# Two weight conversions spread over GpSimd and ScalarE, their raw halves in late token buffers, and three q blocks rotated as one piece

## The chip, the core and the metric

The kernel runs on one core of a Trainium2 chip. The metric is the device time of one execution in microseconds. Lower is better. The five engines of the core are named as in the profile: PE (TensorE; PEld is its weight load), DVE (VectorE), ACT (ScalarE), POOL (GpSimd) and SP (SyncE, which here only issues DMAs).

## The reference, cut to what matters

Attention with rotary position embedding, for 4 batches of 8 heads with 576 positions of 64 channels, and a gated feed-forward layer on its output:

```python
q_rot, k_rot = (rotate(q), rotate(k))
scores = scale * np.matmul(q_rot, k_rot.transpose(0, 1, 3, 2))
scores = scores - np.max(scores, axis=-1, keepdims=True)
attn = np.exp(scores); attn = attn / (np.sum(attn, axis=-1, keepdims=True) + 1e-09)
x = (attn @ v).transpose(0, 2, 1, 3).reshape(2304, 512)
g = x @ w_gate                       # 512 x 1536, random normal
return (g / (1 + np.exp(-g)) * (x @ w_val)) @ w_out
```

The weights of the layer are 64-bit floats. The kernel loads them as pairs of 32-bit words and turns each pair into a 32-bit high part and a low part. This is the conversion that the change is about.

## The kernel before

All products are made from pairs of a high and a low part (fp32r), so each score block takes several matmuls. The kernel has two phases.

**Attention, 0 to 285 us.** The 32 heads are worked in 16 pairs. A pair has nine score blocks of 128x576: n counts blocks over the whole phase, p is the pair and b the block in it (n = 9p + b). For each block PE multiplies (`scores`, L347), DVE takes the negated row maximum (`peak`, L362), ACT takes the exponential (`exp`, L380), PE transposes the result (L423), ACT rounds the transpose to its high part (L424) and DVE subtracts to get the low part (L425). PE then multiplies with v (`pv`, L463), ACT copies the result to Y and SP stores it. Beside this POOL rotates q and k of pair p+2 (`rope`, L200 to L202) and splits v (`vsplit`, L276 and L277). PE transposes the rotated pair p+1 (L287, L291); ACT and DVE split it into the tile N (L306, L310), and SP copies N into the stacked tiles QK, QZ and BD, eight DMAs a pair (`qk_stack`, L317 to L324), which the scores of pair p+1 read. There are two N, QK, QZ and BD, used in turn. From pair 5 on POOL also turns attention outputs that came back from DRAM (Xab, by two DMAs for each piece) and the reciprocal sums (R) into tokens for the second phase (`xprep`, L631 to L634).

**The feed-forward layer, from 285 us on.** It is not touched by the change, but for the two tiles named below that it uses.

The two conversions in the attention phase are for the first block of `w_gate` (i = 0) and of `w_val` (i = 1). `conv` begins each at the first block number of its row in `cv` (the load of the 128x1024 words), and issues one step at each further block number. The steps before are: absolute value (ACT, L733), clamp (DVE, L734), shift (DVE, L735), merge of the exponent into the word (DVE, L736), mask (DVE, L737), rounding to the high part (ACT, L709), product of the low word with the scale (DVE, L738), subtraction and addition (POOL, L711 and L712). All work on 128x512 elements in one tile of the pool `m_r`, which holds a single buffer, named R. The same buffer takes the reciprocal sums later, so the first load of R waits for the last step of the second conversion (L712).

**What sets the order.** PE's order is written out to block 9, SP's to block 46, POOL's to the end of the attention phase. Elsewhere a scheduler places instructions by its own model of time, among what the steps issue. All engines run their streams in order. A DMA on SP also waits until the eighth DMA before it has landed, since they share eight semaphores in turn. All these DMAs go through one queue (q1 in the profile).

The first pair has its own code (`start`): k and block 0 of q are rotated on DVE, the other blocks of q on POOL, with a table that ACT scales first.

Of the kernel before, what the change touches and what calls it, by code (L numbers as in the profile page):

```python
# [10 lines left out]
FP32 = mybir.dt.float32  # L11
F32R = mybir.dt.float32r
U32 = mybir.dt.uint32
ACTF = mybir.ActivationFunctionType
ALU = mybir.AluOpType
AX = mybir.AxisListType

B, H, S, D = 4, 8, 576, 64
# [20 lines left out]
    rope=1,  # L39
    vsplit=8,  # L40
    rstore=0,
    cv=[[9, 13, 14, 15, 16, 17, 17, 19, 24, 24], [28, 36, 37, 38, 39, 40, 40, 42, 44, 44]],
    xs=[[5, 1], [5, 5], [6, 5], [7, 5], [8, 7], [9, 5], [10, 5], [11, 5], [12, 7], [13, 7], [14, 1], [14, 2],
        [14, 8], [15, 0], [15, 2], [15, 4]],
    xe=[[5, 4], [6, 3], [7, 3], [8, 3], [9, 3], [10, 3], [11, 3], [12, 3], [13, 5], [14, 1], [14, 3], [14, 5],
        [15, 1], [15, 3], [15, 5], [15, 7]],
    c1=[[3, 3, 4, 4, 5, 5, 6, 6, 6], [7]],
)
# [39 lines left out]
def bits_f32(x):  # L88
    return float(np.array([x], np.uint32).view(np.float32)[0])


W_LO = bits_f32(896 << 20)
W_HI = bits_f32((1151 << 20) - 1)


def r32(ap):
    return ap.bitcast(FP32)
# [10 lines left out]
class Attn:  # L108
# [101 lines left out]
    def start(self):  # L210
        nc = self.nc
        ve, po = nc.vector, nc.gpsimd
        rot = self.rot[0] = self.rot_p.tile([128, NSLOT, D], FP32, name="rot")
        rf = rot.rearrange("p s d -> p (s d)")
        T = nc.tensor.transpose
        tr = lambda: self.tr_p.tile([128, 512], FP32, name="tr")
        hi = lambda *x: self.qk_hi(0, *x)
        lo = lambda *x: self.qk_lo(0, *x)
        pw = self.pv_p.tile([128, 512], FP32, name="pv")

        def warm(n):
            for _ in range(n):
                nc.tensor.matmul(pw[:, 0:128], self.ident, self.ident, start=True, stop=True)
        w = PLAN["warm"]
        nc.scalar.copy(self.et_p.tile([128, 640], FP32, name="Et")[:, 0:1], r32(self.BD[0])[:, 0, 0:1])
        warm(w[0])
        self.turn(po, 0, 2)
        tp = self.sc_p.tile([128, 1024], FP32, name="sc").rearrange("p (s d) -> p s d", d=D)
        self.turn(ve, 0, 1, 0, 4, tp[:, 0:8])
        nc.scalar.mul(self.tab[0], self.tab[1], float(D ** -0.5))  # L230
        nc.scalar.copy(tp[:, 8:10], self.tab[0][:, :, 0])
        self.turn(ve, 0, 0, 0, 1, tp[:, 10:12], tp[:, 8:10, None])
        self.turn(po, 0, 0, 1, 2)
        self.turn(po, 0, 0, 2, 4)
        pk, pt, pq = tr(), tr(), tr()
        kt = lambda i: T(pk[:, i * 128:(i + 1) * 128], rf[:, 512 + i * 128:640 + i * 128], self.ident)
        for o in (64, 0):
            T(pt[:, o:o + 128], rf[:, 1024:1152], self.ident)
        warm(w[1])
        for i in range(4):  # L240
            kt(i)
        warm(w[2])
        T(pq[:, 0:128], rf[:, 0:128], self.ident)
        for x in ((pt, None, 192), (pk, 640, 512), (pq, 64, 128)):
            hi(*x)
        for x in ((pt, None, 192), (pk, 640, 512), (pq, 64, 128)):
            lo(*x)
        nc.scalar.copy(self.VS[0][:, :, 0:64], self.VR)
        warm(w[3])
        self.scores(0, False, lambda x: warm(w[4]) if x == 0 else None)  # L250
        self.peak(0)
        T(pq[:, 128:256], rf[:, 128:256], self.ident)
        self.scores(1, False)
        self.peak(1)
        hi(pq[:, 128:256], 192, 128)
        self.exp(0)
        lo(pq[:, 128:256], 192, 128)
        self.exp(1)
        warm(w[5])
        self.scores(2)  # L260
        ps = tr()
        for i in range(2, 4):
            T(ps[:, i * 128:(i + 1) * 128], rf[:, i * 128:(i + 1) * 128], self.ident)
        hi(ps[:, 256:512], 320, 256)
        lo(ps[:, 256:512], 320, 256)
        self.exp(2)
        del self.rot[0], self.X[0]
        self.load_qk(2)
        self.qk_stack(0)
# [231 lines left out]
BK = 384  # L501
# [4 lines left out]
class Moe:  # L506
# [197 lines left out]
    def bits10(self, raw, X, hi, lo):  # L704
        nc, po = self.nc, self.nc.gpsimd
        Hf, Xf = r32(raw)[:, :, 1], r32(X)
        ops = self.bits(raw, lo, po, Xf, Xf)
        return ops[:5] + [
            lambda: nc.scalar.copy(hi, Hf),  # L709
            ops[5],  # L710
            lambda: po.tensor_tensor(out=Hf, in0=Hf, in1=r32(hi), op=ALU.subtract),  # L711
            lambda: po.tensor_tensor(out=lo, in0=Hf, in1=Xf, op=ALU.add),  # L712
        ]
# [31 lines left out]

    def wfirst(self, f, i):
        if f == 0:
            tmp = self.r_p.tile([128, 1536], U32, name="R")
        else:
            tmp = self.again("raw0", [128, 1536], U32, "raw")  # L750
        self.nc.sync.dma_start(out=tmp[:, 0:1024], in_=self.wsrc(i, f))
        raw, X = tmp[:, 0:1024].rearrange("p (f t) -> p f t", t=2), tmp[:, 1024:1536]
        if f == 0:
            return self.bits10(raw, X, *self.Wb[f][i])
        go = lambda Xt=None: self.bits9(raw, X, *self.Wb[f][i], self.nc.gpsimd, Xt)
        return (lambda: go(self.aux())) if i else go()
# [215 lines left out]
def attn_swiglu(ctx: ExitStack, tc: tile.TileContext, qk, vr, wg, wv, wo, main, tail, out):  # L972
    nc = tc.nc
# [7 lines left out]
    moe = Moe(tc, keep, pl, yd, rd, hd, wg, wv, wo, out)  # L981
# [3 lines left out]
    ve, po = nc.vector, nc.gpsimd  # L985
# [75 lines left out]
    @step  # L1061
    def x(n, p, b):
        if [p, b] in P["xs"]:
            s, c, t = xq.pop(0)
            need = {8 * s + c, ("r", 2 * s)} | ({4 + c, ("r", 1)} if t else set())
            assert need <= at.done
            if c == 0:
                moe.rload(s, t)
            pend.append((s, c, t, moe.xload(s, c, t)))
        if [p, b] in P["xe"]:  # L1070
            moe.xprep(*pend.pop(0), po)
# [9 lines left out]
    P, cvq, cv1 = PLAN, [], {}  # L1081
# [4 lines left out]
    for n in range(NB):  # L1086
        p, b = divmod(n, 9)
# [24 lines left out]
    ps = [moe.mm(0, 0, 0, 0)]  # L1112
# [9 lines left out]
    ps = [moe.mm(0, 0, 1, 0)]  # L1122
# [258 lines left out]
```

## Time and profile before

| | us |
|---|---|
| median of 3 runs (723.10 to 726.07) | 725.21 |
| the profiled execution | 726.19 |
| its span | 724.4 |

So 1.79 us of the profiled execution lie outside its span, and it is 0.98 us above the median. Over the span PE is busy 97%, DVE 75%, POOL 65% and ACT 57%. The clock that PE was granted is 0.99 of full speed over the span, and 1.00 in every stretch of the attention phase. A pair begins here with its first row maximum on DVE. From pair 7 on most pairs take close to 16.5 us; the earlier ones take between 15.6 and 20.3 us.

### The profile page before, as it was taken

How to read it: one execution, taken by the hardware profiler on the slowest of the kernel's cores; microseconds unless marked ns; L12 is line 12 of the kernel's file. 1: busy time of each engine (PE TensorE's matmuls, PEld its weight loads, DVE VectorE, ACT ScalarE, POOL GpSimd, SP SyncE). 2: the span in 40 equal slices, each digit the busy share in tenths (PEclk: the TensorE clock that was granted, in tenths of full speed). 3: DMA queues.
4: the chain of work that ended last, by engine and by line, in shares of the span. 5: the costliest groups of instructions: out<-in, count | busy, mean ns of one | idle time of the engine just before them, and what ended most of it. 6: DMA issues, size and time to landing. Idle time of an engine off the chain costs nothing.

```text
span 724.4 us, 12748 instructions
## 1 busy us (share of the span) xinstructions
PE 699.1 (97%) x4342; PEld 656.5 (91%) x4342; DVE 541.7 (75%) x889; ACT 409.9 (57%) x891; POOL 472.8 (65%) x473
## 2 busy tenths in 40 slices
PE   7999988999999999997999999999999999999997
PEld 6889988999999998997999999999999877888887
DVE  5798897888888888657998878778667794465451
ACT  5788987888888887346543433415243332432331
POOL 8879699999999858576986766555765767200000
PEclk9999999999999999998999999999999999999999
DMA  4887799779887896873357565745648964787661
GB/s 156 204 226 202 201 235 218 209 206 243 223 224 193 212 217 193 220 248 114 116 150 215 157 177 151 201 133 171 183 122 256 312 231 157 307 279 231 203 218 30
DMA packets 111329, 143.86 MB, mean 199 GB/s; under 512 B 17808, under 2 KB 86048, under 8 KB 111264
## 3 DMA queue, kind: packets, MB, share of 16 engines
q1 hardware_dynamic: 106576, 137.64, 66.6%
q10 hardware_dynamic: 4688, 5.39, 2.2%
q8 instruction: 35, 0.57, 0.3%
q14 instruction: 30, 0.25, 0.1%
HBM read 76.35 MB, written 42.54 MB: 164 GB/s over the span
## 4 chain that ended last, share of the span: by engine, by line
PE 69%; DMA 11%; DVE 8%; ACT 5%; POOL 3%; issue 2%; SPq 2%; ACTq 0%; DVEq 0%; POOLq 0%
PE ch L822 28%; PE ch L939 13%; PE pv L463 9%; PE sc L347 8%; PE tr L423 6%; DMA HF<-hf 3%; PE ch L890 2%; DMA QK<-N 2%; PE tr L287 1%; DMA ht<-sv 1%; ACT E L380 1%; DMA yd<-Y 1%; DMA R<-rd 1%; DVE HF L880 1%; PE ch L774 1%
## 5 line engine op out<-in xcount | busy, mean ns | idle before, releaser
L362 DVE TENSOR_REDUCE nmt<-sc 128x1 f32<-128x576 f32 x144 | 108.2, 752 | 24.4 <-PE sc L347 23.6
L380 ACT ACTIVATE E<-sc,nmt 128x576 f32<-128x576 f32 x128 | 97.1, 759 | 4.5 <-DVE nmt L362 4.5
L423 PE MATMUL tr<-ident,E 128*128 128x128 f32 x512 | 77.2, 273 | 1.1 <-DVE ET1l L425 0.9
L806 POOL TENSOR_TENSOR u<-u,z 128x384 f32<-128x384 f32 x30 | 30.5, 1017 | 71.3 <-DVE sg L806 65.7
L423 PEld LDWEIGHTS tr<-ident,E 128*128 128x128 f32 x512 | 61.4, 141 | 3.9 <-PE tr L287 1.2
L347 PE MATMUL sc<-QK 128*128 128x288 f32 x240 | 58.7, 326 | 4.1 <-DMA QK<-N 2.4
L825 ACT COPY c<-ch 128x384 f32<-128x384 f32 x30 | 14.4, 480 | 84.3 <-PE ch L822 50.2
L200 POOL TENSOR_TENSOR t<-X,tab 128x256 f32<-128x256 f32 (+2 forms) x96 | 55.5, 600 | 6.3 <-DMA X<-in_qk_dram 2.7
L424 ACT CAST ET2h<-tr 128x512 fp32r<-128x512 f32 x80 | 47.0, 588 | 18.0 <-PE tr L423 17.9
L425 DVE TENSOR_TENSOR ET2l<-tr,ET2h 128x512 fp32r<-128x512 f32 x80 | 53.3, 684 | 4.2 <-ACT ET2h L424 3.9
L682 DVE TENSOR_TENSOR hl<-hg,hh 128x384 fp32r<-128x384 f32 x44 | 25.8, 587 | 38.5 <-ACT hh L682 38.5
L939 PE MATMUL ch<-Oh,hh 128*128 128x512 f32 (+1 forms) x144 | 54.0, 375 | 0.0
L939 PE MATMUL ch<-Ol,hh 128*128 128x512 f32 (+1 forms) x144 | 53.8, 374 | 0.0
L939 PE MATMUL ch<-Oh,hl 128*128 128x512 f32 (+1 forms) x144 | 53.8, 374 | 0.0
L347 PE MATMUL sc<-N,QZ 128*128 128x288 f32 x240 | 51.6, 297 | 0.0
L202 POOL TENSOR_TENSOR rot<-rot,t 128x512 f32<-128x512 f32 (+2 forms) x48 | 47.3, 985 | 3.8
L425 DVE TENSOR_TENSOR ET1l<-tr,ET1h 128x512 fp32r<-128x512 f32 x64 | 42.9, 685 | 5.7 <-ACT ET1h L424 5.4
L201 POOL TENSOR_TENSOR rot<-X,tab 128x512 f32<-128x512 f32 (+2 forms) x48 | 47.2, 983 | 0.0
L806 DVE TENSOR_TENSOR sg<-ch,u 128x384 f32<-128x384 f32 x60 | 33.4, 557 | 16.5 <-PE ch L822 13.0
L682 ACT CAST hh<-hg 128x384 fp32r<-128x384 f32 x44 | 22.6, 514 | 38.9 <-DVE hg L926 38.9
L424 ACT CAST ET1h<-tr 128x512 fp32r<-128x512 f32 x64 | 36.9, 595 | 12.1 <-PE tr L423 11.8
L347 PEld LDWEIGHTS sc<-QK 128*128 128x128 f32 x240 | 36.9, 190 | 7.4 <-ACT E L380 3.4
(417 smaller groups left out, 2416.4 us busy)
## 6 DMA issues: line engine op xcount, KB each, us to landing
QK<-N SPq DMA_DIRECT2D x64, 288.0 KB, 4.8
hg<-ht SPq DMA_DIRECT2D x22, 768.0 KB, 6.7
HF<-hf SPq DMA_DIRECT2D x12, 896.0 KB, 5.8
X<-in_qk_dram SPq DMA_DIRECT2D x15, 576.0 KB, 6.4
yd<-Y SPq DMA_DIRECT2D x31, 256.0 KB, 3.3
ht<-sg SPq DMA_DIRECT2D x20, 384.0 KB, 3.6
hf<-sg SPq DMA_DIRECT2D x20, 384.0 KB, 3.4
ht<-sg SPq DMA_DIRECT2D x20, 320.0 KB, 2.9
```

The lines of the kernel that those rows point to most:

```text
L200: e.tensor_tensor(out=sel(t2, u), in0=sel(x, w), in1=tb(Sn, u), op=ALU.mult)
L347: nc.tensor.matmul(ps[:, g, 0:288], l, rr[:, o + g * 288:o + (g + 1) * 288], start=(x == 0), stop=(x == len(terms) - 1))
L362: nc.vector.tensor_reduce(out=nmcol, in_=ps[:, :, 0:288], axis=AX.XY, op=ALU.max, negate=True)
L380: nc.scalar.activation(out=E.rearrange("p (a b) -> p a b", a=2), in_=ps[:, :, 0:288], func=ACTF.Exp, bias=nmcol, scale=1.0, accum_out=self ...
L423: nc.tensor.transpose(ps[:, c], E[:, o + c * 128:o + (c + 1) * 128], self.ident)
L424: nc.scalar.copy(dst[0], src)
L425: nc.vector.tensor_tensor(out=dst[1], in0=src, in1=r32(dst[0]), op=ALU.subtract)
L463: nc.tensor.matmul(st["ps"][:, 0:w], VS[:, sl, :], t, start=(x == 0), stop=(x == last))
L682: return [lambda: self.nc.scalar.copy(h, f), lambda: le.tensor_tensor(out=l, in0=f, in1=r32(h), op=ALU.subtract)]
L806: add = lambda e, out, in0, in1: e.tensor_tensor(out=out, in0=in0, in1=in1, op=ALU.add)
L822: nc.tensor.matmul(acc, l[:, w, c * 128:(c + 1) * 128], r, start=(n == 0), stop=(n == 5))
L939: self.nc.tensor.matmul(ps, l[:, f], r[:, z], start=(n == 0), stop=(n == 3 * NFF - 1))
```

## The change

It has three parts.

1. **Conversion (`bits10`).** The clamp moves from DVE to POOL. The product is taken apart: ACT scales the low word by 2^-52 in place, right after the absolute value, and POOL multiplies. DVE keeps three steps: shift, merge and mask. `cv` gets one more step for each conversion, and the steps move: the first conversion's shift, merge and mask go from blocks 15, 16 and 17 to 18, 21 and 25, the second's from 38, 39 and 40 to 30, 34 and 39. The second conversion's load moves from block 28 to block 20.
2. **Buffers.** The raw words lie in the slots `xa1h` and `xa1l`, tiles for tokens of the third piece (needed from pair 12 on), and no longer in R. The first load of R and of Xab moves from pair 5, block 1 to pair 4, block 6, and the first `xprep` one block earlier.
3. **Start.** ACT scales the small part of the table for block 0 into a PSUM tile of its own (`td`) before it scales the whole table. POOL rotates blocks 1 to 3 of q in one piece. PE transposes them together, and ACT and DVE split them in one 128x384 piece each, in place of one of 128 and one of 256 columns.

```diff
-    cv=[[9, 13, 14, 15, 16, 17, 17, 19, 24, 24], [28, 36, 37, 38, 39, 40, 40, 42, 44, 44]],
-    xs=[[5, 1], [5, 5], ...
+    cv=[[9, 13, 13, 14, 18, 21, 22, 25, 26, 26, 26], [20, 24, 25, 26, 30, 34, 35, 39, 44, 44, 44]],
+    xs=[[4, 6], [5, 5], ...
-    xe=[[5, 4], [6, 3], ...
+    xe=[[5, 3], [6, 3], ...
...
-        tp = self.sc_p.tile([128, 1024], FP32, name="sc").rearrange("p (s d) -> p s d", d=D)
+        tp, td = (self.sc_p.tile([128, 1024], FP32, name="sc").rearrange("p (s d) -> p s d", d=D) for _ in range(2))
         self.turn(ve, 0, 1, 0, 4, tp[:, 0:8])
+        nc.scalar.mul(td[:, 0:2], self.tab[1][:, :, 0], float(D ** -0.5))
         nc.scalar.mul(self.tab[0], self.tab[1], float(D ** -0.5))
-        nc.scalar.copy(tp[:, 8:10], self.tab[0][:, :, 0])
-        self.turn(ve, 0, 0, 0, 1, tp[:, 10:12], tp[:, 8:10, None])
-        self.turn(po, 0, 0, 1, 2)
-        self.turn(po, 0, 0, 2, 4)
+        self.turn(ve, 0, 0, 0, 1, tp[:, 8:10], td[:, 0:2, None])
+        self.turn(po, 0, 0, 1, 4)
...
-        T(pq[:, 128:256], rf[:, 128:256], self.ident)
+        ps = tr()
+        for i in range(1, 4):
+            T(ps[:, i * 128:(i + 1) * 128], rf[:, i * 128:(i + 1) * 128], self.ident)
         self.scores(1, False)
+        hi(ps[:, 128:512], 192, 384)
+        lo(ps[:, 128:512], 192, 384)
         self.peak(1)
-        hi(pq[:, 128:256], 192, 128)
         self.exp(0)
-        lo(pq[:, 128:256], 192, 128)
...
-        ps = tr()
-        for i in range(2, 4):
-            T(ps[:, i * 128:(i + 1) * 128], rf[:, i * 128:(i + 1) * 128], self.ident)
-        hi(ps[:, 256:512], 320, 256)
-        lo(ps[:, 256:512], 320, 256)
...
-        return ops[:5] + [
+        return [
+            ops[0],
+            lambda: nc.scalar.mul(r32(L), L, 2.0 ** -52),
+            lambda: po.tensor_scalar(out=Xf, in0=Xf, scalar1=W_LO, scalar2=W_HI, op0=ALU.max, op1=ALU.min),
+            ops[2], ops[3],
             lambda: nc.scalar.copy(hi, Hf),
-            ops[5],
+            ops[4],
+            lambda: po.tensor_tensor(out=Xf, in0=r32(L), in1=Xf, op=ALU.mult),
             lambda: po.tensor_tensor(out=Hf, in0=Hf, in1=r32(hi), op=ALU.subtract),
...
-            tmp = self.r_p.tile([128, 1536], U32, name="R")
+            tmp = self.again(f"xa1{'hl'[i]}", [128, 1536], U32, "raw")
...
+            if (s, t, c) == (0, 2, 0):
+                assert not cvq
+                moe.xa[1] = [moe.again(f"xa1{x}", [128, 4, BK], F32R, f"xa1{x}") for x in "hl"]
```

On PE at the start, before (L347 are the scores of blocks 0, 1 and 2, L252 the transpose of q's block 1, L263 those of blocks 2 and 3, L423 the first transposes of exponentials, L223 filling matmuls):

```order
L347 MATMUL sc<-N_93 128x288 x6
L252 MATMUL tr<-ident,rot 128x128
L347 MATMUL sc<-N_93 128x288 x6
L223 MATMUL pv<-ident 128x128
L347 MATMUL sc<-N_93 128x288 x6
L263 MATMUL tr<-ident,rot 128x128 x2
L423 MATMUL tr<-ident,E 128x128 x4
```

The same place after the change, where the transposes of the three blocks are L253 and the scores L343:

```order
L343 MATMUL sc<-N_93 128x288 x6
L253 MATMUL tr<-ident,rot 128x128 x3
L343 MATMUL sc<-N_93 128x288 x6
L223 MATMUL pv<-ident 128x128
L343 MATMUL sc<-N_93 128x288 x6
L419 MATMUL tr<-ident,E 128x128 x4
```

All three transposes now stand between the scores of blocks 0 and 1, and nothing of q is left behind the scores of block 2.

On DVE at the turn from pair 1 to pair 2, before (L734 to L737 are the clamp, shift, merge and mask of the first conversion):

```order
L734 TENSOR_SCALAR R<-R 128x512
L362 TENSOR_REDUCE nmt<-sc 128x1
L425 TENSOR_TENSOR ET2l<-tr,ET2h 128x4x128
L735 TENSOR_SCALAR R<-R 128x512
L362 TENSOR_REDUCE nmt<-sc 128x1
L425 TENSOR_TENSOR ET2l<-tr,ET2h 128x4x128
L736 SCALAR_TENSOR_TENSOR R<-R 128x512
L362 TENSOR_REDUCE nmt<-sc 128x1
L425 TENSOR_TENSOR ET2l<-tr,ET2h 128x4x128
L737 TENSOR_SCALAR R<-R 128x512
```

On DVE in pair 2 after the change (L737 is now the shift, L738 the merge; L358 and L421 are the row maximum and the low part):

```order
L435 TENSOR_TENSOR TK2l<-tr,TK2h 128x384
L737 TENSOR_SCALAR raw<-raw 128x512
L358 TENSOR_REDUCE nmt<-sc 128x1
L306 TENSOR_TENSOR N_113<-tr,N_113 128x512
L421 TENSOR_TENSOR ET1l<-tr,ET1h 128x4x128
L358 TENSOR_REDUCE nmt<-sc 128x1
L421 TENSOR_TENSOR ET1l<-tr,ET1h 128x4x128
L358 TENSOR_REDUCE nmt<-sc 128x1
L421 TENSOR_TENSOR ET1l<-tr,ET1h 128x4x128
L738 SCALAR_TENSOR_TENSOR raw<-raw 128x512
L421 TENSOR_TENSOR ET1l<-tr,ET1h 128x4x128
```

Four steps in a row, one a block, have left the end of pair 1; in pair 2 several blocks lie between two steps.

On SP in pairs 4 and 5, before, from the load of X for pair 7 to the last QK of pair 6 (L617 is the first load of R; the two loads of Xab before it stand 31 and 44 rows earlier):

```order
L169 DMA X<-in_qk_dram 128x1152
L180 DMA VR<-in_vr_dram 128x640
L487 DMA yd_58<-Y_1307 128x2x256
L488 DMA yd_58<-Y_1307 128x2x64
L482 DMA yd_57<-Y_1435 128x2x256
L169 DMA X<-in_qk_dram 128x1152
L617 DMA R<-rd 64x4x384 x2
L319 DMA QZ_96<-N_93 64x512
L322 DMA QZ_96<-N_93 64x512
L323 DMA BD_95<-N_93 64x2x64
L324 DMA BD_95<-N_93 64x2x64
L180 DMA VR<-in_vr_dram 128x640
```

The same stretch after the change (L613 is the load of R, L620 are the loads of Xab):

```order
L169 DMA X<-in_qk_dram 128x1152
L180 DMA VR<-in_vr_dram 128x640
L483 DMA yd_58<-Y_1308 128x2x256
L484 DMA yd_58<-Y_1308 128x2x64
L613 DMA R<-rd 64x4x384 x2
L620 DMA Xab<-yd_57 64x2x384 x4
L478 DMA yd_57<-Y_1433 128x2x256
L169 DMA X<-in_qk_dram 128x1152
L315 DMA QZ_96<-N_93 64x512
L318 DMA QZ_96<-N_93 64x512
L319 DMA BD_95<-N_93 64x2x64
L320 DMA BD_95<-N_93 64x2x64
```

In both, the four QK copies of pair 6 come next (before, right behind the last row shown; after, behind one VR load more). R has moved ahead of a store of Y and a load of X, and four loads of Xab that stood much earlier now stand behind it. The load of `w_val`, which stood ahead of the X and VR loads of pair 3, stands after the change between the X and VR loads of pair 2.

## Rows read from the trace of the kernel before

**Rows 1.** Stretches: pair 1, pairs 2 and 3, pairs 4, 5, 6, and pair 9 (last).
```profile
core 0: us, PE busy (x) PEld busy (x) DVE busy (x) ACT busy (x) POOL busy (x), PEclk, DMA share, GB/s
29.42:48.67 19.25, 18.55 (x141) 17.23 (x142) 16.69 (x26) 15.64 (x38) 13.76 (x16) 1.00 0.89 222
48.67:80.95 32.28, 31.39 (x243) 29.79 (x242) 28.68 (x49) 28.73 (x73) 26.62 (x30) 1.00 0.80 200
80.95:101.29 20.34, 18.74 (x146) 17.64 (x144) 19.57 (x31) 17.00 (x43) 14.76 (x16) 1.00 0.80 225
101.29:117.89 16.60, 15.00 (x115) 14.37 (x116) 13.48 (x23) 14.59 (x38) 15.87 (x20) 1.00 1.04 227
117.89:135.26 17.37, 16.57 (x131) 15.99 (x130) 14.38 (x23) 13.90 (x36) 16.56 (x20) 1.00 0.90 231
168.40:184.88 16.48, 16.38 (x131) 15.97 (x130) 14.41 (x23) 14.58 (x39) 15.65 (x20) 1.00 0.94 234
```

**Rows 2.** DVE's busy time in the steps of both conversions, 28 to 101 us.
```profile
28.00:101.00 73.00, 8.88 (x10) 1.00 0.82 212
```

**Rows 3.** Groups of DVE, 28 to 110 us: clamp and product of the conversions.
```profile
L738 DVE SCALAR_TENSOR_TENSOR R<-R 128x512 f32<-128x512 uint32 x2 | 1.9, 970 | 0.0
L734 DVE TENSOR_SCALAR R<-R 128x512 f32<-128x512 f32 x2 | 1.9, 950 | 0.0
```

**Rows 4.** Timeline of POOL and DVE near 44 us: start, duration, instruction.
```profile
43.72 1.29 POOL L201 TENSOR_TENSOR rot<-X,tab 128x512 f32<-128x512 f32 x1
...
43.81 1.48 DVE L734 TENSOR_SCALAR R<-R 128x512 f32<-128x512 f32 x1
...
46.48 0.41 DVE L735 TENSOR_SCALAR R<-R 128x512 uint32<-128x512 uint32 x1
```

**Rows 5.** Timeline of pair 0: DVE, SP and PE.
```profile
8.05 0.23 DVE L200 TENSOR_TENSOR sc<-X,sc 128x64 f32<-128x64 f32 x1 [0.40 <-ACT sc L231]
...
14.63 0.73 SPq L317 DMA_DIRECT2D QK<-N  x1
...
23.37 0.37 PE L347 MATMUL sc<-QK 128*128 128x288 f32 x1 [1.24 <-DMA QK<-N]
```

**Rows 6.** Last QZ copy of pair 2 on SP, and the scores that read it.
```profile
42.93 1.27 SPq L322 DMA_DIRECT2D QZ<-N  x1
...
48.68 0.50 PE L347 MATMUL sc<-QK 128*128 128x288 f32 x2
```

**Rows 7.** DMA issues near 40.7 and 33.4 us: count, size, us to landing.
```profile
QZ<-N SPq DMA_DIRECT2D x1, 128.0 KB, 3.6
...
R<-in_moe_w_gate_dram SPq DMA_DIRECT2D x1, 512.0 KB, 8.6
```

**Rows 8.** Timeline at the turn from pair 2 to pair 3: SP and ACT.
```profile
61.76 0.37 SPq L180 DMA_DIRECT2D VR<-in_vr_dram  x1
...
66.46 0.76 ACT L380 ACTIVATE E<-sc,nmt 128x576 f32<-128x576 f32 x1
```

**Rows 9.** Groups of ACT and POOL, 28 to 110 us.
```profile
L733 ACT ACTIVATE R<-R 128x512 f32<-128x512 f32 x2 | 1.4, 690 | 0.2 <-DMA R<-in_moe_w_gate_dram 0.2
...
L711 POOL TENSOR_TENSOR R<-R,w1h 128x512 f32<-128x512 f32 x1 | 1.3, 1325 | 0.0
...
L276 POOL TENSOR_SCALAR VS<-VR 128x640 fp32r<-128x640 f32 x5 | 3.9, 778 | 11.3 <-DMA VR<-in_vr_dram 11.3
```

**Rows 10.** The wait for QK at the end of pair 5: chain, then PE.
```profile
109.17 7.78 DMA QK<-N
...
117.09 0.50 PE L347 MATMUL sc<-QK 128*128 128x288 f32 x2 [1.16 <-DMA QK<-N]
```

**Rows 11.** SP's own waits, 84 to 118 us: total, times, longest.
```profile
SPq L482 <- ACT Y L468: 1.8, 1, 1.8
...
SPq L617 <- POOL w1l L712: 0.9, 1, 0.9
```

**Rows 12.** The DMA queue of SP, 84 to 118 us: packets, MB, share.
```profile
q1 hardware_dynamic: 5234, 7.42, 90.6%
```

More of the change, by code (lines that the diff above doesn't have):

```diff
@@ L41 @@
     rstore=0,
-    cv=[[9, 13, 14, 15, 16, 17, 17, 19, 24, 24], [28, 36, 37, 38, 39, 40, 40, 42, 44, 44]],
-    xs=[[5, 1], [5, 5], [6, 5], [7, 5], [8, 7], [9, 5], [10, 5], [11, 5], [12, 7], [13, 7], [14, 1], [14, 2],
+    cv=[[9, 13, 13, 14, 18, 21, 22, 25, 26, 26, 26], [20, 24, 25, 26, 30, 34, 35, 39, 44, 44, 44]],
+    xs=[[4, 6], [5, 5], [6, 5], [7, 5], [8, 7], [9, 5], [10, 5], [11, 5], [12, 7], [13, 7], [14, 1], [14, 2],
         [14, 8], [15, 0], [15, 2], [15, 4]],
-    xe=[[5, 4], [6, 3], [7, 3], [8, 3], [9, 3], [10, 3], [11, 3], [12, 3], [13, 5], [14, 1], [14, 3], [14, 5],
+    xe=[[5, 3], [6, 3], [7, 3], [8, 3], [9, 3], [10, 3], [11, 3], [12, 3], [13, 5], [14, 1], [14, 3], [14, 5],
         [15, 1], [15, 3], [15, 5], [15, 7]],
@@ L706, in bits10 @@
         Hf, Xf = r32(raw)[:, :, 1], r32(X)
+        L = raw[:, :, 0]
         ops = self.bits(raw, lo, po, Xf, Xf)
-        return ops[:5] + [
+        return [
[3 more added lines that the diff above has]
+            ops[2], ops[3],
             lambda: nc.scalar.copy(hi, Hf),
-            ops[5],
+            ops[4],
+            lambda: po.tensor_tensor(out=Xf, in0=r32(L), in1=Xf, op=ALU.mult),
             lambda: po.tensor_tensor(out=Hf, in0=Hf, in1=r32(hi), op=ALU.subtract),
```

## The prediction

> **What bounds the kernel now.** I read the page first, then busy time by stretch, one stretch for each head pair, then the timelines, waits and chain of the stretches that are too long. The page puts PE at 97% and the chain mostly on PE. A steady pair shows what that means: 16.48 us with PE busy for 16.38 of them, the last of [rows 1]. There nothing on another engine is worth anything. The first seven pairs are different. Pair 1 takes 19.25, pairs 4 and 5 together 36.94 against 32.96 for two steady pairs, pair 6 17.37; pairs 2 and 3 take 32.28 and are not slow [rows 1]. So the change can only earn in the start, pairs 0 and 1, and pairs 4 to 6. Whatever it earns there carries to the end, since PE's work behind it is the same and in the same order.
>
> In pair 1 and pair 4 DVE is the full engine: 16.69 of 19.25 and 19.57 of 20.34 [rows 1]. The ten DVE steps of the two conversions are 8.88 us of it [rows 2]. Pair 5 is another case: DVE has 3.1 us to spare, the DMA share is 1.04 [rows 1], and at its end PE waits 1.16 us for QK, which was 7.78 us on the way [rows 10].
>
> **The change, part by part.** Signs are those of the time.
>
> *Start, -0.4.* DVE waits 0.40 us for ACT's copy of the scaled table [rows 5], which had stood behind DVE's own k rotation because both write one tile. With a tile of its own the wait goes. Bounds: 0 (POOL's merged rotation is late for the three transposes) to -0.6.
>
> *Pair 0, -1.2.* SP starts the QK copies at 14.63, behind the split of q's last blocks, and PE then waits 1.24 us for QK [rows 5]. Now all three blocks are split right after the first scores, about two score blocks earlier, some 2.5 us. That is more than the wait, so all of it goes, less a little for the three transposes that now stand ahead of the second scores. Bounds: 0 to -1.5.
>
> *Pair 1, -1.4.* Of the 2.77 us over a steady pair, some 0.5 are four extra matmuls (18.55/141 = 0.13 each, two blocks with six in place of four), which stay. The other 2.2 are DVE's: the clamp, shift, merge and mask leave the pair. What is late next is QZ: its copy is issued at 42.93 and read by the scores at 48.68 [rows 6]. Landing as fast as the one before it, 3.6 us [rows 7], it gives 2.1 us of room; the issue itself took 1.27, so the queue was full and I count 1.4. Bounds: -0.4 to -2.2.
>
> *Pairs 2 and 3, +1.0.* They take the steps that left pair 1. DVE keeps 8.88 less clamp and product, 1.9 each [rows 2, 3], so about 5.0 for six steps, 0.84 each. Four of the six now fall here in place of two, mask and product: about 1.7 more on DVE, 30.4 of 32.3, which fits. A step costs 0.41 with POOL idle and 1.48 when it starts just behind a 1.29 us POOL instruction: it waits that one out [rows 4]. The Trainium skill (SBUF — State Buffer, Who interferes with whom) states the same: DVE's two-port instructions and GpSimd share a port pair, and the second to start blocks for the whole instruction. By it the shift and mask stay exposed and moving the clamp to POOL only lengthens POOL's hold; the trace agrees on the wait. ACT has 28.73 of 32.28 and gets about two steps of 0.69 more [rows 1, 9]. The new wait is on ACT: `w_val` now leaves where the VR load stood, 61.76, and ACT reaches its absolute value after the exponential at 66.46, at about 67.2 [rows 8]. Landing like `w_gate`, 8.6 us after its issue [rows 7], it holds ACT for 3.1 us, with the exponentials behind it; landing within 5.4 it holds nothing. I take 1.0 for all this. Bounds: 0 to +3.1.
>
> *POOL, 0 in the sum.* It gains per conversion a clamp, 778 x 512/640 = 620 ns by the VS row, and a product of 1.32 [rows 9], so 3.9 in all. POOL is busy for 26.62 of 32.28 in pairs 2 and 3 and 30.63 of 36.94 in pairs 4 and 5 [rows 1], which holds it; what it cannot hold is a rival below. The Trainium skill (GPSIMD Engine Reference, Engine selection) speaks against the move: two-input elementwise work belongs on VectorE and is about twice as slow on GpSimd. The trace has 1.32 against 0.97 with DVE's waits in it [rows 3, 9], so the direction agrees and the price is smaller here.
>
> *Pairs 4 and 5, +0.2.* DVE loses four of five steps of the second conversion in pair 4. Alone that would be worth up to 36.94 - 32.96 = 4.0. I do not count it, because the end of pair 5 is set by the DMA queue and not by DVE. The QK copies of pair 6 are last in a queue that is full since the middle of pair 4. The change puts four Xab loads into it, 64x2x384 words or 0.197 MB each, 0.79 MB. The queue moves 7.42 MB in 34 us, 0.218 MB/us [rows 12]: 3.6 us more ahead of QK. Two things give time back. SP's R load no longer waits 0.9 us for the conversion's last step, nor behind the store that waited 1.8 for Y [rows 11]: 2.7 us. And the absolute value, 0.69 on ACT [rows 9], leaves the path to the tile N that SP waits for early in pair 4. 3.6 - 2.7 - 0.7 = +0.2. PE will be ready earlier in pair 5 and stand about 3 us at its end, where it now stands 1.16. Bounds: -4.0 (QK in time) to +3.6 (nothing given back).
>
> *Pair 6 and behind, 0.* POOL's and the queue's backlog is the same kind as before.
>
> Sum: -0.4 - 1.2 - 1.4 + 1.0 + 0.2 = -1.8. The profiled execution, 726.19 with a span of 724.4, becomes 724.4. It lies 0.98 above the median of the runs, so I forecast 723.4 for the median.
>
> **The rivals.**
>
> *A: DVE was all of it.* QK of pair 6 lands in time, and pairs 4 and 5 take 33.4, near two steady pairs. For it: DVE is full in pair 4 and idles least where the steps stand [rows 1]; SP may issue everything some 3 us earlier against PE than I allow. Against it: the share of 1.04 with a later wait for QK [rows 1, 10] and 0.79 MB more. Pairs 2 and 3 then cost 0.4 in place of 1.0, and pairs 4 and 5 give 3.5: -0.4 - 1.2 - 1.4 + 0.4 - 3.5 = -6.1, so 719.1.
>
> *B: the queue is the bound, twice; slower.* One mechanism: a load put ahead of what is waited for. `w_val` holds ACT for the full 3.1 at pair 3, 2.1 over what I count, and the Xab loads cost their full 3.6 at pair 6's QK, 3.4 over: -1.8 + 2.1 + 3.4 = +3.7, so 728.9. It turns the change into a loss from 1.8 us of such waits beyond mine. For it: the 8.6 us of `w_gate` and the 7.78 us of QK. Against it: `w_val` has no queue as full as `w_gate` had (share 0.80 against 0.89).
>
> *C: POOL's stream is late.* The product, subtraction and addition now follow each other in front of the next VS and rotation, so rotations come 1.9 us later after each conversion, and PE's transposes of the rotated pair wait: up to 3.8, -1.8 + 3.8 = +2.0, so 727.2. Against it: POOL's 5.7 and 6.3 us of idle time in the two stretches.
>
> **How the numbers follow.** Chances: my forecast 0.47, A 0.38, B 0.10, C 0.05. About 0.5%, 3.6 us, is what a measurement here can tell from no change. My forecast alone spans 721.0 to 726.5 and is nearly all within that; A is nearly all beyond it on the fast side, and a little of my forecast's low end joins it: faster 0.40, same 0.49, slower 0.11 (B and part of C). The range has to take in A as well as the high end of my forecast: 718.0 to 727.0. That leaves out A's best end and B.
>
> **What would show it.** Right: DVE's 0.40 wait and PE's 1.24 wait in pair 0 are gone; pair 1 near 17.8; conversion steps on DVE about 5 us in six; PE waiting 2 to 4 us for QK at the end of pair 5, with pairs 4 and 5 still near 37 us. Wrong: pairs 4 and 5 near 33 us and no such wait (A); ACT idle for `w_val` at the start of pair 3 and a QK wait over 5 us (B); PE or SP waiting for POOL's rotations (C). A change behind pair 7 would contradict the claim that the rest is carried over unchanged.

## The result, and the profile after

The changed kernel takes 729.08 us (median of 10 runs, 726.10 to 732.76) against 725.09 for the kernel before in the same job (721.77 to 727.84). The ratio is 1.0063 with an interval of 1.0034 to 1.0092: slower by 4 us, against a forecast of 1.8 faster. The profiled execution of the changed kernel is the longest of its ten, 732.76 with a span of 731.0, so the traces are 6.6 us apart where the medians are 4.0.

The stretches of [rows 1] in the changed kernel, cut at the same events: pair 1, pairs 2 and 3, pairs 4, 5 and 6, and pair 10.

```profile
core 0: us, PE busy (x) PEld busy (x) DVE busy (x) ACT busy (x) POOL busy (x), PEclk, DMA share, GB/s
27.42:49.25 21.83, 18.77 (x133) 17.83 (x134) 14.76 (x23) 16.03 (x39) 17.55 (x20) 0.92 0.90 227
49.25:83.66 34.41, 32.86 (x254) 31.27 (x253) 31.79 (x50) 30.05 (x73) 27.57 (x31) 1.00 0.66 165
83.66:101.39 17.73, 16.97 (x132) 16.00 (x131) 15.74 (x29) 15.86 (x40) 15.58 (x17) 1.00 0.67 165
101.39:124.54 23.15, 16.68 (x128) 16.13 (x128) 14.35 (x25) 14.99 (x39) 19.79 (x26) 0.92 1.04 265
124.54:142.57 18.03, 17.91 (x131) 17.50 (x130) 14.47 (x23) 14.02 (x36) 16.62 (x21) 0.91 0.76 201
175.71:192.20 16.49, 16.39 (x131) 15.98 (x130) 14.41 (x24) 14.59 (x39) 15.17 (x19) 1.00 1.00 254
```

Against [rows 1], pair 1 is 2.6 us longer, pairs 2 and 3 are 2.1 longer, pair 4 is 2.6 shorter, pair 5 is 6.6 longer and pair 6 0.7 longer. From pair 7 to the end it is 588.4 us for 589.1. In pairs 1 and 4 DVE is no longer full; in pairs 2 and 3 it is fuller than before (31.79 of 34.41 us, from 28.68 of 32.28). Most of the loss lies in pairs 1 and 5, where PE stands and the granted clock is 0.92; pair 6 has 0.91.

**Pair 0** takes 16.52 us in place of 18.38. The answer to [rows 5], on DVE, SP and PE:

```profile
7.77 0.49 DVE L200 TENSOR_TENSOR sc<-X,sc 128x64 f32<-128x64 f32 x2
...
11.88 0.73 SPq L313 DMA_DIRECT2D QK<-N  x1
...
21.56 0.52 PE L343 MATMUL sc<-QK 128*128 128x288 f32 x2
```

The QK copies start 2.75 us earlier, and neither DVE nor PE waits.

**Pair 1.** ACT's wait for its absolute value, the answer to the first row of [rows 9]; then the gap on PE.

```profile
42.11 0.66 ACT L735 ACTIVATE raw<-raw 128x512 f32<-128x512 f32 x1 [2.31 <-DMA raw<-in_moe_w_gate_dram]
42.68 0.65 ACT L707 ACTIVATE raw<-raw 128x512 f32<-128x512 uint32 x1
...
44.58 1.06 PE L343 MATMUL sc<-N,BD 128*128 128x288 f32 x6 [2.64 <-ACT E L376]
```

The stretch behind the gap, with the columns of the first table:

```profile
47.20:49.25 2.05, 2.05 (x11) 2.03 (x11) 0.27 (x1) 0.79 (x4) 0.45 (x2) 0.50 0.46 140
```

The pair starts 2.0 us earlier, but `w_gate` lands at 42.1, where it landed at 42.0 before: its load was issued 1.35 us earlier (32.09 for 33.44) and took 10.0 us in place of 8.6. ACT reaches the step early and stands, and the next exponential stands behind it, with the scaling's 0.65 on top. PE idles 2.64 us and, from some 1.3 us behind the gap on, runs at the lower clock (0.50, 1.2 GHz).

**The end of pair 5.** SP's stream from the R load to the QK copies of pair 6, and PE's first score block with them; this answers to [rows 10].

```profile
101.27 1.98 SPq L613 DMA_DIRECT2D R<-rd  x2
103.30 2.57 SPq L620 DMA_DIRECT2D Xab<-yd  x4
105.97 0.59 SPq L478 DMA_DIRECT2D yd<-Y  x1
...
107.94 0.50 SPq L315 DMA_DIRECT2D QZ<-N  x1
...
114.25 0.60 SPq L313 DMA_DIRECT2D QK<-N  x1
114.94 0.70 SPq L314 DMA_DIRECT2D QK<-N  x1
...
123.20 0.82 PE L343 MATMUL sc<-QK 128*128 128x288 f32 x2 [6.36 <-DMA QK<-N]
```

The stretch behind that wait:

```profile
123.20:126.00 2.80, 2.80 (x12) 2.78 (x13) 1.36 (x2) 0.61 (x2) 2.64 (x7) 0.50 1.02 313
```

PE waits 6.36 us where it waited 1.16 [rows 10], and comes back at the lower clock. SP's own waits there (engine, line, releaser: total, times, longest):

```profile
SPq L318 <- DMA R<-rd: 1.2, 1, 1.2
...
SPq L315 <- DMA R<-rd: 0.8, 1, 0.8
SPq L313 <- DMA Xab<-yd: 0.7, 1, 0.7
```

The QZ copies wait for the two R loads to land and the first QK copy for an Xab load. Each of these is the eighth DMA ahead of the one that waits. So the Xab loads can make the QK copies late in three ways: by the bytes that they put ahead of them, by the 2.57 us that SP needs to issue them, and by their places among the eight. SP's waits for their landing come to 1.4 us in all (0.3, 0.2 and 0.2 beside the 0.7).

### The profile page after: what moved, and what is told of

It reads as the page before. It is cut to its first block, busy times and chain, and to the rows that moved or that the text cites. A ratio compares the mean times of both kernels' runs of the same rounds, so it can differ in the third digit from the quotient of the medians.

```text
span 731.0 us, 12751 instructions
## 1 busy us (share of the span) xinstructions
PE 700.2 (96%) x4342; PEld 658.1 (90%) x4342; DVE 541.9 (74%) x884; ACT 410.4 (56%) x892; POOL 477.1 (65%) x473
## 4 chain that ended last, share of the span: by engine, by line
PE 69%; DMA 10%; DVE 7%; ACT 6%; POOL 4%; issue 2%; SPq 1%; ACTq 0%; POOLq 0%; DVEq 0%
PE ch L824 27%; PE ch L941 13%; PE pv L459 9%; PE sc L343 7%; PE tr L419 6%; PE ch L892 3%; DMA raw<-in_moe_w_gate_dram 3%; DMA HF<-hf 2%; ACT E L376 1%; PE tr L283 1%; DMA ht<-sv 1%; POOL t L200 1%; DMA QK<-N 1%; ACT N L302 1%; POOL rot L201 1%
## 5 line engine op out<-in xcount | busy, mean ns | idle before, releaser
L358 DVE TENSOR_REDUCE nmt<-sc 128x1 f32<-128x576 f32 x144 | 108.2, 752 | 30.2 <-PE sc L343 29.2
L343 PE MATMUL sc<-QK 128*128 128x288 f32 x240 | 59.5, 329 | 7.7 <-DMA QK<-N 6.4
L421 DVE TENSOR_TENSOR ET2l<-tr,ET2h 128x512 fp32r<-128x512 f32 x80 | 53.4, 684 | 6.4 <-ACT ET2h L420 6.3
L343 PE MATMUL sc<-N,QZ 128*128 128x288 f32 x240 | 51.8, 298 | 0.0
L421 DVE TENSOR_TENSOR ET1l<-tr,ET1h 128x512 fp32r<-128x512 f32 x64 | 43.0, 685 | 6.1 <-ACT ET1h L420 5.8
L343 PEld LDWEIGHTS sc<-QK 128*128 128x128 f32 x240 | 37.4, 193 | 10.8 <-issue 6.6
L808 DVE TENSOR_TENSOR sg<-ch,u 128x384 f32<-128x384 f32 x60 | 33.4, 557 | 16.2 <-PE ch L824 13.0
```

The source lines that it names most:

```text
L343: nc.tensor.matmul(ps[:, g, 0:288], l, rr[:, o + g * 288:o + (g + 1) * 288], start=(x == 0), stop=(x == len(terms) - 1))
L358: nc.vector.tensor_reduce(out=nmcol, in_=ps[:, :, 0:288], axis=AX.XY, op=ALU.max, negate=True)
L421: nc.vector.tensor_tensor(out=dst[1], in0=src, in1=r32(dst[0]), op=ALU.subtract)
L808: add = lambda e, out, in0, in1: e.tensor_tensor(out=out, in0=in0, in1=in1, op=ALU.add)
```

## The experiments

Theories: *the queue* (the first R and Xab loads stand ahead of pair 6's QK copies in a full queue), *ACT's wait* (conversion steps on ACT stand for a weight load, the exponentials behind them), *POOL* (its stream is late, with the clamp at 1.92 us). Ratios are to the kernel before in the same job; where no ratio is given, the kernel was executed once, with a profile.

**Loads back where they were** (`e1_xab_back`, changed kernel)

```diff
-    xs=[[4, 6], [5, 5], ...      xe=[[5, 3], [6, 3], ...
+    xs=[[5, 1], [5, 5], ...      xe=[[5, 4], [6, 3], ...
```

> The changed kernel with the first R and Xab loads and their use back at pair 5, blocks 1 and 4, where they stood before. Theory (the queue: four Xab loads of 0.79 MB and the R load stand ahead of the QK copies of pair 6): the 6.4 us wait of PE for QK at the end of pair 5 falls to under 2, pairs 4 and 5 fall from 40.9 us to about 36, and the time by 4 to 5 us, to 724-725. Rival (POOL is late, since its clamp takes 1.92 us and the products stand ahead of the next rotation): the copies of QK are late anyway, the wait stays over 5 us and the time falls by less than 1 us.

Measured: 723.73, ratio 0.9966 [0.9939, 0.9993]. Pairs 4 to 6, with the columns of the first table:

```profile
83.55:101.27 17.72, 16.95 (x131) 15.99 (x131) 15.77 (x29) 15.84 (x40) 15.53 (x17) 1.00 0.77 191
101.27:118.07 16.80, 16.44 (x128) 15.68 (x127) 14.34 (x25) 14.17 (x38) 13.04 (x16) 1.00 0.96 249
118.07:134.52 16.45, 16.34 (x131) 15.94 (x130) 14.41 (x23) 14.57 (x39) 15.72 (x20) 1.00 0.80 211
```

The two entries are worth 1.0063 - 0.9966, about 1% or 7 us, more than the whole loss. (Where both kernels ran in one job, `e2_abs_late` and `e3_both` below, the same two entries are worth 5.5 us.) The table's entries do not say when a load leaves: block 42 lies in the part of SP's stream that is written out (to block 46), where the loads stand behind the stores of pair 4. From pair 5 on the scheduler places them, and it puts R at 90.10 and the first Xab loads between 49 and 71 us:

```profile
50.62 0.60 SPq L620 DMA_DIRECT2D Xab<-yd  x1
...
69.57 1.26 SPq L620 DMA_DIRECT2D Xab<-yd  x2
...
90.10 1.27 SPq L613 DMA_DIRECT2D R<-rd  x2
```

POOL falls as the cause of the wait: PE, DVE, ACT and POOL have the same instructions in the same order as in the changed kernel from start to end, only SP's order differs, and the wait is gone.

**R late, Xab back** (`e7_R_late_alone`: as e1, with R's load alone at pair 4, block 6)

```diff
+        if [p, b] == [4, 6]:
+            moe.rload(0, 0)
```

> The changed kernel with only the R load left at pair 4, block 6, in SP's written order; the first two Xab pairs go back to pair 5, where the scheduler may issue them as soon as their rows are stored. Theory (bytes ahead of QK in a full queue, 0.79 MB of R and 0.79 MB of Xab of some 3 us each): the wait for QK at the end of pair 5, 6.4 us with both and 0.2 with neither, comes out at 2 to 4 us; time about halfway between the changed kernel and the one with the loads back, 726. Rival (one of the two alone does it): under 1 us or over 5.

Measured: 723.39, ratio 0.9987 [0.9966, 1.0008]. SP's stream behind R, and PE at the end of pair 5:

```profile
98.20 1.49 SPq L613 DMA_DIRECT2D R<-rd  x2
100.43 0.37 SPq L478 DMA_DIRECT2D yd<-Y  x1
...
107.41 1.46 SPq L314 DMA_DIRECT2D QK<-N  x1
```

```profile
114.81 0.50 PE L343 MATMUL sc<-QK 128*128 128x288 f32 x2 [1.05 <-DMA QK<-N]
```

That is the wait of the kernel before, under the 2 to 4 expected. Here R leaves 17.6 us after the start of pair 4, exactly as in the changed kernel, and the four Xab loads in SP's order are all that differs. PE starts on QK 34.2 us after the start of pair 4 in place of 39.5. So the four Xab loads cost 5.3 us.

Where these are spent can be read from the store of Y that stands right behind the Xab loads, and that did not wait for a place. From its issue to its landing, first with the Xab loads ahead of it, then here:

```profile
yd<-Y SPq DMA_DIRECT2D x1, 256.0 KB, 8.7
```

```profile
yd<-Y SPq DMA_DIRECT2D x1, 256.0 KB, 6.8
```

Counted from the start of pair 4 it lands at 31.05 us in place of 26.67. So 4.4 of the 5.3 us are lost by the time this store has landed, which no place held back and which stands ahead of every QZ and QK copy of pair 6: the transfers of the loads themselves take them. That leaves at most 0.9 us for the eight places.

**R earlier, Xab late** (`e8_Xab_late_alone`: the changed kernel with R's load at pair 4, block 2)

> The changed kernel with only the R load earlier, at pair 4, block 2, so that it leaves before the stores of pair 4 that SP waits for; the four Xab loads stay at pair 4, block 6. Theory (bytes): the wait for QK at the end of pair 5 comes out at 2 to 4 us, time about 726. Rival (Xab alone does it): 5 to 6.5 us and a time near the changed kernel's. Rival (R alone does it): under 1 us.

PE at the end of pair 5:

```profile
118.11 0.82 PE L343 MATMUL sc<-QK 128*128 128x288 f32 x2 [4.49 <-DMA QK<-N]
```

4.49, just above the bytes theory's 2 to 4, and a time that no theory had: 732.87, ratio 1.0118 [1.0088, 1.0148]. R went only 1.5 us ahead of pair 5, so this did not take it out of the way. The rest of the loss lies behind the last pair, where this edit also reordered SP's stream: 462.2 us from pair 15 to the end against 456.2 in the changed kernel. Which DMA costs it there stays open, and I do not use its total.

**Half the Xab loads** (`e6_half_Xab`, changed kernel)

```diff
-        if n == 46:
+        if n == 51:
             ctl0.__exit__(None, None, None)
```

> The changed kernel with SP's written order kept for five blocks more (until block 51 for 46), so that two Xab loads stand ahead of pair 6's QK copies in place of four, the second two behind them; the QK copies also stand ahead of the QZ copies. Theory (what counts is what stands ahead of the copies): the wait at the end of pair 5, 6.4 us with four and 1.1 with none, comes out at 1.5 to 4. Rival (the kind of load, not how many): still over 5.

PE at the end of pair 5:

```profile
116.55 0.50 PE L343 MATMUL sc<-QK 128*128 128x288 f32 x2 [1.72 <-DMA QK<-N]
```

723.71, and a wait of 1.72: PE starts on QK 35.0 us after the start of pair 4, so two loads cost under 1 us over none (34.2), four 5.3. The QK copies also stand ahead of the QZ copies here, so the wait is not clean on how the cost grows. The store behind the loads stands where it stood: it lands 28.2 us after the start of pair 4, 1.5 later than with none and 2.9 earlier than with four. The rival, that any such load costs over 5 us, falls.

**First conversion's ACT steps later** (`e2_abs_late` on the changed kernel, `e3_both` with the loads back too)

```diff
-    cv=[[9, 13, 13, 14, 18, ...
+    cv=[[9, 15, 15, 16, 18, ...
```

> The changed kernel with the first conversion's absolute value and scaling two blocks later on ACT (blocks 15 and 15 for 13 and 13), its clamp two blocks later on POOL; the w_gate load stays. Theory (ACT stands 2.3 us for w_gate with the next exponential behind it, PE 2.6 us, and PE runs slower behind the gap): pair 1 falls from 21.8 us to 18 to 19. At the end part is given back, since pair 6's QK is set by the queue: 1 to 3 us of the time. Rival (something else of pair 1 is late, the QZ copies or the VR load): pair 1 stays over 20.5 us.

> Both edits: first R and Xab loads back at pair 5, and the first conversion's absolute value and scaling two blocks later. Theory: pair 1 at 18 to 19 us and pairs 4 and 5 at about 36: 7 to 8 us under the changed kernel, 721 to 722, some 0.5% under the kernel before. Rival (POOL is late): pairs 4 and 5 stay at 39 or more and the time is over 725.

Measured: 728.57, ratio 1.0042 [1.0022, 1.0062], and 723.05, ratio 0.9965 [0.9940, 0.9990]. Pair 1 is 18.25 and 18.26 us, as ACT's wait has it. The time gains little over the kernels without this edit (1.0063 and 0.9966, inside the intervals), and `e3_both` misses the 0.5% under the kernel before that I expected. In both traces ACT then stands at the next load, `w_val` at the start of pair 3: here in `e3_both`, ACT and PE, and then the stretch behind PE's gap.

```profile
64.69 0.68 ACT L735 ACTIVATE raw<-raw 128x512 f32<-128x512 f32 x1 [1.03 <-DMA raw<-in_moe_w_val_dram]
...
66.66 0.41 PE L429 MATMUL tr<-ident,E 128*128 128x128 f32 x2 [1.78 <-DVE N L306]
```

```profile
69.00:72.00 3.00, 3.00 (x16) 2.98 (x15) 2.22 (x5) 2.14 (x5) 2.85 (x5) 0.59 0.76 194
```

Pair 3 is 19.3 us there and 18.5 in `e2_abs_late`, against 17.1 in the changed kernel.

**Second conversion's ACT steps later too** (`e5_val_late`, on `e3_both`)

```diff
-    ... 25, 26, 26, 26], [20, 24, 25, 26, 30, ...
+    ... 25, 26, 27, 27], [20, 24, 25, 27, 30, ...
```

> The kernel of both edits (loads back at pair 5, first conversion's ACT steps at block 15) with the second conversion's absolute value, scaling and clamp one block later, block 27, behind ACT's two copies into N. There ACT stood 1.03 us for w_val and 1.1 us with the two steps, PE 1.8 us for N, and PE ran at half clock for some 5 us behind it; pair 3 took 19.4. Theory (the in-order wait on ACT and the clock behind the gap make pair 3 long): pair 3 falls to 16.5 to 17.5, pair 7 starts 2 us earlier than in the kernel of both edits, the ratio goes to 0.993-0.994. Rival (POOL's late stream makes pair 3 long: products and the clamp ahead of VS): pair 3 stays over 18.5.

Measured: 722.76. Pair 3:

```profile
62.72:78.87 16.15, 16.15 (x128) 15.58 (x128) 14.58 (x26) 15.51 (x40) 15.26 (x17) 1.00 0.79 209
```

Pair 3 falls to 16.15 with PE never idle: ACT's wait again. The ratio, 0.9976 [0.9956, 0.9996], is not what I expected, and can't be told from that of `e3_both`: pair 7 starts 1.4 us earlier in its trace, and the span is 0.9 longer.

**Clamp back on DVE** (`e9_clamp_on_dve`, on `e5_val_late`)

> The kernel of e5_val_late with the clamp of both conversions back on VectorE; GpSimd, where it took 1.92 us each, loses it. If POOL's stream holds anything: pair 2 or pair 4 gets shorter by up to 2 us. If POOL is covered: within 0.5 us of e5_val_late, or slower by up to 1 us, since DVE gets 1.9 us more work and waits for the port.

Measured: 722.26, ratio 0.9964 [0.9940, 0.9989]; the same as `e5_val_late` within the intervals. The traces do not agree with that: pair 2 is 15.95 us in place of 17.15 and pair 4 17.55 in place of 18.56, the sign that I had set for a POOL stream that holds something. One trace each does not settle it: in the seven traces named at the end, pair 2 took 16.27 to 17.29 with the same instructions on PE, DVE, ACT and POOL. So whether POOL's clamp is covered stays open.

**The parts alone** (`e4_start_alone`: the kernel before with the new start; `e10_conv_alone` and `e13_conv_again`: with the new conversion)

> The kernel before with the changed start alone: the scaled table in a tile of its own, one rotation of q's last three blocks on POOL, their split right behind the first scores. If the start's gain in pair 0 (1.9 us in the trace of the changed kernel) carries to the end: ratio 0.9975. If the queue at pair 5 sets the end and not what comes before it: 1.000 and a QK wait at the end of pair 5 longer by the gain, 3 us in place of 1.2.

> The kernel before with the changed conversion alone: the start and the lists of the token loads are the old ones. By the runs so far (start alone 0.9978, start and conversion 0.9966) the conversion is worth little: ratio 0.997 to 1.001. If the conversion is what costs (ACT's wait for w_gate in pair 1, POOL's clamp): over 1.003.

> The changed conversion alone once more, for a second trace. If pair 0's 21.1 us there (QK landing 1.1 us later than in the kernel before, PE standing 2.35 us and then at half clock) is built in: pair 0 again over 20.5. If it is one execution's landing: 18.3 to 18.8, as in both traces of the kernel before. Pair 3, with ACT's wait for w_val and two steps ahead of N: 17 to 19.5 either way.

The start alone: 724.06, ratio 0.9978 [0.9957, 1.0000]; pair 0 is 16.52 and PE waits 2.23 us for QK at the end of pair 5, against 1.16 and 1.81 in the two traces of the kernel before. The interval holds both 0.9975 and 1.000, so how much is given back there can't be told. The conversion alone: 728.45, ratio 1.0042 [1.0014, 1.0070], slower, and 727.49 in a second execution. That is the time that I had set for a conversion that costs, over 1.003, but not at the place: pair 1 is 18.01 us in the first of its traces. The two have pair 0 at 21.06 and 22.35 us against 18.38 and 18.34 in the kernel before. In the first PE stands 2.35 us for QK and comes back at the lower clock; in the second it runs at the lower clock from 14 us on, with no such gap ahead:

```profile
14.00:26.00 12.00, 12.00 (x48) 10.18 (x48) 6.86 (x11) 6.21 (x15) 11.53 (x17) 0.50 0.70 154
```

With the new start pair 0 is 16.5 to 17.0 in all twelve traces that have it. So the parts don't add up. But in pair 0 all five engines have the same instructions in the same order here as in the kernel before; the conversion's own work begins in pair 1. What made pair 0 longer, and why the clock fell there with the same start that ran at full clock before, stays open.

**Second traces** (`e11_after_again`, `e12_before_again`, `e14_xab_back_again`)

> The changed kernel once more, for a second trace. Kernels with the same instructions on every engine up to pair 3 had pair 1 at 18.0, 19.2, 21.8 and 22.0 us, with ACT standing 0, 1.1, 2.3 and 2.4 us for w_gate. Theory (that wait varies with the execution, the one at the end of pair 5 is built in): pair 1 anywhere from 18 to 22, the wait for QK at the end of pair 5 again 5 to 7 us. Rival (both are built in): pair 1 again 21.5 to 22.

> The kernel before once more, for a second trace: the wait for QK at the end of pair 5 again 0.5 to 3 us, pair 1 at 18.5 to 20.5, the sum of the first seven pairs within 2 us of the first trace's 124.2.

> The changed kernel with the first R and Xab loads back at pair 5, once more: no wait for QK at the end of pair 5 over 0.5 us (built in), pair 1 anywhere from 18 to 22 (by w_gate's landing).

The wait for QK is built in: 6.24 in the second trace of the changed kernel, 1.81 in that of the kernel before, none at the end of pair 5 with the loads back. Pair 1 is not fixed: 19.87 in the second trace of the changed kernel, 19.38 with the loads back. Pairs 4 and 5 of the kernel before took 35.4 in place of 36.9, and pair 1 18.12, where I had expected 18.5 to 20.5; its first seven pairs took 120.6, 3.6 less than in the first trace, where I had allowed 2. The times of these three executions are 728.38, 725.64 and 722.64 us; the kernel before, once in the same job as the last of them, took 721.61. The ten runs of either kernel in the first comparison lie 6 to 7 us apart, so single times do not say which kernel is faster. Pairs 1 and 4 in the second trace of the kernel before:

```profile
29.70:47.82 18.12, 17.69 (x139) 16.96 (x140) 15.88 (x26) 15.39 (x38) 13.79 (x16) 1.00 0.85 220
80.10:98.23 18.13, 18.05 (x145) 17.50 (x144) 17.35 (x31) 16.82 (x43) 13.05 (x15) 1.00 0.78 211
```

## Why the prediction was wrong

- **Pairs 4 and 5, +0.2: the step that failed.** The mechanism was the one named, the queue ahead of QK, and both sides of the sum 3.6 - 2.7 - 0.7 were mis-sized.

  The cost: the four Xab loads, put at 3.6 us by bytes over the queue's mean rate, cost 5.3 with all else equal. 4.4 of these are the loads' own transfers (0.79 MB at 0.18 MB/us where I took 0.218), and at most 0.9 come from SP's eight places, which the sum left out.

  What was given back: less than the 3.4 counted. R does leave 17.6 us after the start of pair 4 in place of 20.6, and pair 4 is 2.6 us shorter. But with R alone late PE starts on QK 34.2 us after the start of pair 4, against 36.1 and 34.6 in the two traces of the kernel before: 1.9 and 0.4 given back. Against the first trace that makes 5.3 - 1.9 = +3.4 at QK, where the sum had +0.2.

  PE stood 6.36 in place of "about 3", and the lower clock behind the gap cost another 1.6 us in pair 6 (18.03 against 16.45 with the loads back), which I had at 0. Pairs 4 and 5 took 40.9 us against my 37, beyond the bound of +3.6. At pair 6's QK that is rival B's mechanism, to which I gave 0.10. One reading was wrong without weight in the sum: DVE lost three of the five steps of the second conversion in pair 4, not four.
- **Pair 1, -1.4: wrong in sign** (+2.6 in the first pair of traces, +1.8 in the second). DVE did lose the work (14.76 busy for 16.69), and where ACT did not stand, with R alone late, the pair took 18.01 us, near the 17.85 that the sum gives. What is late next is not QZ but `w_gate` on ACT. I had its 8.6 us and ACT's wait of 0.2 for it in front of me [rows 7, 9], and the start term made ACT 2 us earlier at a load that did not land earlier. Rival B looked for this wait at `w_val` only, and there ACT did not stand in either trace of the changed kernel.
- **Pairs 2 and 3, +1.0: low.** They took 2.1 us more in the first pair of traces and 1.2 in the second, inside the bounds. DVE's six steps are 6.13 us in place of 5.0, and the four that fall here 4.80 where 1.25 stood before, 3.6 more for the 1.7 counted. First the busy time of the six, then the shifts alone (shortest, median and longest in ns). Both shifts start just behind a POOL instruction of 1.3 us, as in [rows 4]:

```profile
28.00:101.00 73.00, 6.13 (x6) 0.98 0.73 182
```

```profile
L737 DVE TENSOR_SCALAR raw<-raw x2: 1393/1438/1483, 54.3 to 78.4; 128x512 uint32<-128x512 uint32 x2
```

- **POOL, 0: not contradicted,** though a term of it was wrong and `e9_clamp_on_dve` leaves it open. The clamp takes 1.92 us, three times the 0.62 that I took from the VS row:

```profile
L708 POOL TENSOR_SCALAR raw<-raw x2: 1917/1918/1920, 45.3 to 70.8; 128x512 f32<-128x512 f32 x2
```

  The Trainium skill (GPSIMD Engine Reference, Engine selection) has one-input work on GpSimd at roughly line rate; this clamp of 512 elements is slower than the two-input product (1.32), so for it the measurement decides against the page.
- **Start, -0.4, and pair 0, -1.2: right in sum** (-2.0 us). DVE's and PE's waits [rows 5] are gone, but the start itself is only 0.14 us shorter and pair 0 1.86, beyond its bound of 1.5. The start alone is worth 0.22%, with an interval that reaches 1.0000.
- **All but pairs 4 and 5** was forecast at -2.0 us. With the loads back, the rest of the change measures -0.34%, -2.5 us. That agreement is luck. In the trace with the loads back pair 1 lost 2.8 us and pairs 2 and 3 lost 1.9; the gains were 1.8 in pair 0, and 2.4 in pairs 4 and 5 and 0.9 in pair 6, which the -2.0 leaves out.

The best versions, with the loads back (`e1_xab_back`, and with ACT's steps later `e3_both` and `e9_clamp_on_dve`), are all 0.35% faster than the kernel before and 1% faster than the changed one; among themselves they can't be told apart.

## What to carry to other kernels

A load made earlier in a table can become later: look at which loads and stores it then stands between in its queue's stream. Bytes over the mean rate of the queue gave 3.6 us where 5.3 were measured, so take the price of a load from landings around such a load where a trace has them. When a gain ahead of a transfer's landing moves an in-order engine forward but not the transfer, the engine stands there with all that is queued behind it; go through each DMA wait of the old trace, however short, and ask by how much its reader now comes sooner. A forecast that rests on one trace should allow for what a second would show.

## What the runs showed that I had not expected

- The same instructions do not give the same pair 1. Seven traces share every stream through pair 1 (changed kernel twice, loads back twice, R late, R earlier, half the loads). ACT stood 0.00 to 2.40 us for `w_gate` in them, and pair 1 took 18.01 to 22.03 us. With R alone late the load took 7.8 us to land, with the loads back 10.0 and 9.0.
- A gap on PE of some 2.7 us did not always bring the lower clock. In the half-load kernel PE idled 2.71 us at the same place and came back at full clock; with the loads back it idled 2.73 and came back at 0.56. The two stretches, the first from the half-load kernel:

```profile
44.77:46.80 2.03, 2.03 (x16) 2.03 (x17) 1.41 (x2) 1.92 (x6) 1.95 (x2) 1.00 0.94 172
```

```profile
44.53:47.00 2.47, 2.47 (x12) 2.45 (x13) 1.45 (x2) 1.43 (x4) 2.38 (x2) 0.56 0.81 186
```

- Why the transfers of four Xab loads hold the store behind them back by 4.4 us and those of two by 1.5 is not settled.
